# A retention, Mish and squared-ReLU kernel on one core: weights loaded in their own order, odd heads moved by ScalarE, decays broadcast by TensorE, and new constants in the planner

## The chip, the cores and the metric

The kernel runs on one core of one Trainium2 chip. The metric is the device time of one launch in microseconds (us). The kernel before took 871.28 us (median of 3 runs, 869.62 to 871.64). Engines are named as in the profile: PE is TensorE (PEld its weight loads), DVE is VectorE, ACT is ScalarE, POOL is GpSimd, and SP (SyncE) issues every DMA.

## The reference, cut to what matters

```python
# 1. retention: q, k, v of shape (4, 8, 576, 64), float32
scores = (1 / np.sqrt(64)) * np.matmul(q, k.transpose(0, 1, 3, 2))
gamma = 1.0 - 2.0 ** (-5.0 - np.arange(8))
rel = pos[:, None] - pos[None, :]
Dmat = np.where(rel >= 0, gamma[:, None, None] ** rel[None], 0.0)
x = np.matmul(scores * Dmat[None], v)                 # heads side by side: (2304, 512)
# 2. first feed-forward layer: w_in (512, 2048), w_out (2048, 512)
h = x @ w_in
x = (h * np.tanh(softplus(h))) @ w_out                # Mish
# 3. second feed-forward layer, with weights of its own
h = np.maximum(x @ w_in2, 0.0)
out = (h * h) @ w_out2
```

The input weights reach the kernel as the 64-bit words of the host's arrays, and the kernel turns them into float32 itself.

## The kernel before, in words

**Retention.** It goes through 20 steps, five for each batch: four chunks of 128 tokens and a tail of 64. For a step TensorE makes the scores of eight heads (`scores`, L449), VectorE multiplies them with a table of decays (`a`, L458), TensorE makes the outputs from the running state and from the chunk itself (`apply`, L501 and L510) and updates the state (`update`, L471). The keys are scaled with `vdec_sb` (`scale_k`) and the queries with `qdec_sb` (`scale_q`), on VectorE or GpSimd. The table `decay` is made once at the start (`make_decay`): two DMAs repeat a row of `qdec` on all 128 partitions, and eight VectorE instructions (L418) multiply it with a column of `vdec_sb` and the causal mask.

Heads lie in pairs: an even pair has its two heads in partitions 0 to 63 and 64 to 127; for an odd pair `out` gives the upper half of PSUM to the first head and the lower half to the second. ScalarE copies both banks as they are into `part` (two copies a chunk of tokens), so that in `part` the odd pairs have their halves exchanged. To match, the rows of the first layer's `w_in` are loaded with the same exchange by `swapped`: three DMAs, one of 256 KB over all partitions, and two of 128 KB that bring 64 partitions each from the other half. All other weights come as one DMA of 512 KB.

**Weights.** `convert` turns one block of 64-bit words into a float32 tile: a ScalarE copy of the low words (`y`), three VectorE instructions on the high words (`z`, L293 to L295), a VectorE instruction that joins them (`y`, L296), and an addition on VectorE or GpSimd (L297). There are two `raw` buffers, so block i waits until block i-2 has been read. `split_in` and `split_out` cut the tiles into high and low parts for float32r matmuls. Sixteen of the 64 blocks are `w_in` of the first layer.

**Feed-forward layers.** The tokens go in three visits of 768 through four passes over the hidden width, for each of the two layers: 24 visits. `chain` makes seven products for each pair of hidden blocks (L652) in place of eight, with sums of inputs and weights made beforehand; `y_group` makes the second matmul (L702). The split inputs of a visit (`ring`) are kept in DRAM (`keep`) and come back in later passes (`fetch`, 768 KB each).

**The planner.** The order on every engine is made before launch by `Plan`. Each operation has an assumed cost; `due` counts back from when TensorE would need it; `order` simulates the five queues and picks, for each engine, the ready operation that is due first (TensorE only the first ready of the next 14). A DMA costs SP 0.45 us, moves its bytes at an assumed 0.39 MB/us through one queue, and is taken as landed 2.0 us after that. DMAs are issued at most 4 us of queue ahead (`BACKLOG`). Weight DMAs are due 20 us before they are needed (`EARLY`). The engines then run their instructions in the planned order, each with the semaphore waits that its data asks for, so an instruction that waits holds all that stand behind it on its engine.

At the start eleven matmuls on a zero tile (`WARM`) run before the first scores. The launch order asked for there is: step 0, mask, vdec, the decays, step 1, the first 256 columns of `qdec`, steps 2 and 3, the rest of `qdec`; the planner is free to issue them by due time.

Of the kernel before, what the change touches and what calls it, by code (L numbers as in the profile page):

```python
# [54 lines left out]
NEAR = 0.5  # L55
SHARE = 0.8
GATE = 6
EARLY = 20.0
LAST = 14


class Plan:
# [6 lines left out]
    def __init__(self):  # L69
        self.ops, self.wrote, self.read, self.early = [], {}, {}, []  # L70

    def add(self, eng, cost, fn, reads=(), writes=(), moved=0.0, port=False, early=0.0):
# [15 lines left out]
        self.early.append(early)  # L88
        return i

    def due(self):
        due = [1e9] * len(self.ops)
        t = 0.0
        for i, (costs, *_) in enumerate(self.ops):
            if "PE" in costs:
                due[i] = t
                t += costs["PE"]
        for i in range(len(self.ops) - 1, -1, -1):
            for d in self.ops[i][2]:
                costs, _, _, moved, _ = self.ops[d]  # L100
                e = min(costs, key=costs.get)
                c = costs[e] + SEEN[e] + (moved + 2.0 if e == "SP" else 0.0)
                due[d] = min(due[d], due[i] - c)
        return [d - e for d, e in zip(due, self.early)]

    def order(self):
# [6 lines left out]
        free = dict.fromkeys(self.ENGINES, 0.0)  # L113
        ready, start, on = [0.0] * n, [0.0] * n, [None] * n
        waiting = {e: [] for e in self.ENGINES}
# [10 lines left out]
        for i in range(n):  # L126
            if not left[i]:
                release(i)
        queue = 0.0
        for _ in range(n):  # L130
# [3 lines left out]
            for e in self.ENGINES:  # L134
# [3 lines left out]
                if not c:  # L138
                    continue
                now = max(free[e], min(ready[i] for i in c))  # L140
                if e == "SP":
                    now = max(now, queue - BACKLOG)
                can = [i for i in c if ready[i] <= now + 1e-9]
                if e == "POOL":
# [32 lines left out]
            if eng == "SP":  # L177
                queue = max(queue, end) + moved
                end = queue + 2.0
            for u in users[i]:  # L180
                ready[u] = max(ready[u], end + (0.0 if eng == "PE" and "PE" in ops[u][0] else seen))
                left[u] -= 1
                if not left[u]:
                    release(u)
        self.end = max(free.values())
# [10 lines left out]
def kernel(  # L196
# [55 lines left out]

    def dma(out, in_, reads, writes, size, early=0.0):
        fn = lambda: nc.sync.dma_start(out=out, in_=in_)
        plan.add("SP", 0.45, fn, reads, writes, size / 0.39e6, early=early)

    def swapped(out, in_, reads, writes, size, early=0.0):

        a, b = slice(0, D), slice(D, P)
        dma(out[:, 0::2], in_[:, 0::2], reads, writes[:1], size / 2, early)  # L260
        dma(out[a, 1::2], in_[b, 1::2], reads, writes[1:2], size / 4, early)
        dma(out[b, 1::2], in_[a, 1::2], reads, writes[2:], size / 4, early)

# [13 lines left out]
    def convert(i, after=()):  # L277
        g, a = halves[i]
        r, z, y = raw[i % RAWS], zs[i % 2], ys[i % YS]
        kr, kz, ky = [("raw", i % RAWS, j) for j in range(3)], ("z", i % 2), ("y", i % YS)  # L280
        made[g, a] = y, ky
        src = (wp1, wp2)[g // NF].bitcast(U32)[g % NF, a]
        if g < NF and a == 0:
            to, of = (t.rearrange("p (k n) -> p k n", k=KD) for t in (r.rearrange("p n w -> p (n w)"), src))
            swapped(to, of, after, kr, P * DM * 8, EARLY)
        else:
            dma(r.rearrange("p n w -> p (n w)"), src, after, kr, P * DM * 8, EARLY)
        low, hi = r[:, :, 0], r[:, :, 1]
# [140 lines left out]
    def scale_q(s):  # L429
        b, c = steps[s]  # L430
        if not c:
            return
        q, t = heads(s)[:, 0], slice(c * CH, c * CH + size(c))
        either(ALU.mult, q, q, qdec_sb[:, :, t], NP * size(c), [("qdec", int(c > 1)), ("q", s % LD)], [("q", s % LD)])

# [4 lines left out]
    def scores(s):  # L440
# [13 lines left out]
        for e in range(2):  # L454
# [3 lines left out]
                lambda e=e, r=r, d=d: nc.vector.tensor_tensor(a[r, e, :, :n], ps[r, e, :, :n], d, op=ALU.mult),  # L458
                NP * n, [("decay", e), ("sc", s % 2, e)], [("a", s % 2, e)],
            )  # L460
# [22 lines left out]
    def apply(s):  # L483
# [46 lines left out]
    zero = cst.tile([P, 512], F32R, tag="zero", name="zero")  # L530
    warm = pso[2].rearrange("p h t -> p (h t)")
# [37 lines left out]
    def open_late():  # L569
# [18 lines left out]
             + [("e", j) for j in range(ES)] + ["mask", "vdec", "zero"]  # L588
             + [("qdec", i) for i in range(2)] + [("decay", e) for e in range(2)])

# [92 lines left out]
    def y_group(u, th, f):  # L683
# [7 lines left out]
        for i in range(na):  # L691
# [15 lines left out]

            plan.add("PE", 0.52 if m == 0 else 0.69, mm, [kw + (0,), kw + (1,), ("g", j, 0), ("g", j, 1), ky], [ky])
        if f < FPP - 1:
# [138 lines left out]
```

## Time and profile before

| | before |
|---|---|
| median of 3 runs | 871.28 us |
| the profiled execution's own time | 870.46 us |
| its span, first to last instruction | 868.7 us |
| PE busy | 830.3 us (96%) |
| DVE busy | 612.1 us (70%) |
| ACT busy | 404.0 us (47%) |
| POOL busy | 130.1 us (15%) |
| mean granted TensorE clock | 0.986 |
| moved by DMA | 191.94 MB, 221 GB/s |

Busy time is what an engine's instructions cover; DMA-issuing instructions are not in it. Matmuls are pipelined and their ends are modelled, so a busy PE is not a PE at its peak. The span is 1.76 us shorter than the execution's time. Retention takes the first 92 us of the span, the feed-forward layers the rest.

### The profile page before, as it was taken

The numbers are of one execution on the slowest core, as the hardware profiler recorded it, in microseconds if no ns is written. First come the engines' busy times: TensorE is split into PE (matmuls) and PEld (weight loads), VectorE is DVE, ScalarE is ACT, GpSimd is POOL, SyncE is SP. The second block draws the span as 40 slices with busy tenths as digits, with TensorE's granted clock in tenths as the row PEclk, the third lists the DMA queues.
The fourth block names the chain that finished last, engine by engine and source line by source line (L and its number), as shares of the span: only waits on it lengthen the run. The fifth ranks groups of instructions, "written<-read, shape, count | busy, mean of one in ns | idle before, by whom it ended". The sixth has DMA issues, their size and how long they took to land.

```text
span 868.7 us, 13459 instructions
## 1 busy us (share of the span) xinstructions
PE 830.3 (96%) x5195; PEld 774.3 (89%) x5195; DVE 612.1 (70%) x1082; ACT 404.0 (47%) x817; POOL 130.1 (15%) x91
## 2 busy tenths in 40 slices
PE   7877889998999999999999999999999999999998
PEld 6766779998999999999999989888889889889986
DVE  4799999748437673677549998779468964664453
ACT  1423665655335433554347557564344533543331
POOL 1544360011001100112000321110011201000000
PEclk7989999999999999999999999999999999999999
DMA  9988565686375574477357376468348536426621
GB/s 326 325 287 320 204 262 194 243 299 232 120 278 189 186 303 172 156 278 295 125 211 278 107 293 252 151 233 323 122 172 312 195 157 255 177 99 270 263 101 73
DMA packets 50944, 191.94 MB, mean 221 GB/s; under 512 B 5440, under 2 KB 15808, under 8 KB 50880
## 3 DMA queue, kind: packets, MB, share of 16 engines
q1 hardware_dynamic: 50880, 191.08, 60.5%
q8 instruction: 41, 0.67, 0.3%
q14 instruction: 23, 0.19, 0.1%
HBM read 153.31 MB, written 37.75 MB: 220 GB/s over the span
## 4 chain that ended last, share of the span: by engine, by line
PE 68%; DVE 17%; DMA 7%; ACT 3%; issue 3%; POOL 1%; SPq 0%; DVEq 0%; POOLq 0%; ACTq 0%
PE py L702 35%; PE h L652 30%; DMA raw<-in_wp_dram 5%; DVE y L296 2%; DVE g L265 1%; DVE z L293 1%; DVE z L294 1%; DVE a L458 1%; PE o L510 1%; DVE part L725 1%; DVE z L295 1%; DVE y L297 1%; DVE win L250 1%; PE sc L449 1%; DMA kv<-in_kv_dram 1%
## 5 line engine op out<-in xcount | busy, mean ns | idle before, releaser
L652 PE MATMUL h<-ring,win 128*128 128x384 f32 x2016 | 386.4, 337 | 12.8 <-ACT cp L242 9.4
L652 PEld LDWEIGHTS h<-ring,win 128*128 128x128 f32 x2016 | 356.1, 188 | 25.0 <-ACT cp L242 13.1
L702 PE MATMUL py<-g,wout 128*128 128x384 f32 x1152 | 216.6, 335 | 1.6 <-DVE part L725 0.9
L702 PE MATMUL py<-wout,g 128*128 128x512 f32 x864 | 214.8, 393 | 0.0
L702 PEld LDWEIGHTS py<-g,wout 128*128 128x128 f32 x1152 | 200.6, 188 | 3.8 <-DVE part L725 2.1
L702 PEld LDWEIGHTS py<-wout,g 128*128 128x128 f32 x864 | 161.0, 188 | 29.8 <-DVE g L265 0.4
L242 ACT ACTIVATE cp<-h 128x384 f32<-128x384 f32 x144 | 70.8, 492 | 120.4 <-PE h L652 117.5
L265 DVE TENSOR_TENSOR g<-h,g 128x384 fp32r<-128x384 f32 x144 | 79.4, 551 | 31.5 <-ACT g L242 31.2
L297 POOL TENSOR_TENSOR y<-z,y 128x512 uint32<-128x512 uint32 x35 | 51.4, 1469 | 281.8 <-DVE y L296 237.6
L242 ACT ACTIVATE g<-h 128x384 fp32r<-128x384 f32 x144 | 70.6, 491 | 41.0 <-DVE h L611 39.1
L635 DVE TENSOR_TENSOR e<-h,cp 128x384 f32<-128x384 f32 x48 | 26.6, 554 | 76.6 <-ACT cp L242 76.6
L725 DVE TENSOR_TENSOR part<-py,part 128x384 f32<-128x384 f32 (+1 forms) x126 | 73.3, 606 | 6.5 <-PE py L702 5.4
L635 DVE TENSOR_TENSOR h<-h,cp 128x384 f32<-128x384 f32 x96 | 53.9, 562 | 31.5 <-PE h L652 30.6
L242 ACT ACTIVATE h<-h 128x384 f32<-128x384 f32 x72 | 34.2, 476 | 67.2 <-DVE h L635 54.6
L242 ACT ACTIVATE e<-h 128x384 f32<-128x384 f32 x72 | 35.2, 489 | 52.6 <-DVE h L635 45.9
L242 ACT ACTIVATE y<-raw 128x512 f32<-128x512 uint32 x64 | 43.0, 671 | 28.8 <-DVE wout L250 8.8
L296 DVE SCALAR_TENSOR_TENSOR y<-raw,y 128x512 uint32<-128x512 uint32 x64 | 45.9, 721 | 7.5 <-ACT y L242 7.5
L293 DVE TENSOR_SCALAR z<-raw 128x512 uint32<-128x512 uint32 x64 | 31.3, 489 | 26.7 <-DMA raw<-in_wp_dram 26.5
L611 DVE SCALAR_TENSOR_TENSOR h<-h,e 128x384 f32<-128x384 f32 x72 | 40.3, 560 | 11.4 <-ACT e L242 11.3
L250 POOL TENSOR_TENSOR win<-y,win 128x512 fp32r<-128x512 f32 x9 | 12.1, 1349 | 223.8 <-ACT win L242 220.0
L265 DVE TENSOR_TENSOR g<-e,g 128x384 fp32r<-128x384 f32 x48 | 29.4, 612 | 19.6 <-ACT g L242 19.6
L242 ACT ACTIVATE e<-e 128x384 f32<-128x384 f32 x48 | 25.2, 524 | 31.8 <-DVE e L635 31.8
(51 smaller groups left out, 649.7 us busy)
## 6 DMA issues: line engine op xcount, KB each, us to landing
ring<-d SPq DMA_DIRECT2D x126, 768.0 KB, 6.7
d<-ring SPq DMA_DIRECT2D x42, 768.0 KB, 5.2
raw<-in_wp_dram SPq DMA_DIRECT2D x48, 512.0 KB, 3.6
qk<-in_qk_dram SPq DMA_DIRECT2D x16, 512.0 KB, 7.4
kv<-in_kv_dram SPq DMA_DIRECT2D x16, 512.0 KB, 7.7
out_dram<-part SPq DMA_DIRECT2D x18, 256.0 KB, 2.1
raw<-in_wp_dram SPq DMA_DIRECT2D x16, 256.0 KB, 3.7
raw<-in_wp_dram SPq DMA_DIRECT2D x32, 128.0 KB, 4.7
```

The costliest lines, as they stand in the source:

```text
L242: fn = lambda: nc.scalar.activation(out() if callable(out) else out, in_() if callable(in_) else in_, func, **kw)
L250: fn = lambda eng: eng.tensor_tensor(get(out), a, get(b).bitcast(F32), op=op)
L265: return lambda: eng.tensor_tensor(out, a, b.bitcast(F32), op=ALU.subtract)
L293: dve(lambda: ts(z, hi, 0x7FFFFFFF, None, op0=band), 256, kr, [kz], True)
L294: dve(lambda: ts(zf, zf, HI_MIN, HI_MAX, op0=ALU.max, op1=ALU.min), 256, [kz], [kz], True)
L296: dve(lambda: stt(yu, hi, 0x80000000, yu, op0=band, op1=bor), 512, kr + [ky], [ky], True)
L297: add = lambda eng: eng.tensor_tensor(yu, z, yu, op=ALU.add)
L611: lambda: nc.vector.scalar_tensor_tensor(ph(), ph(), 0.0, e(), op0=ALU.max, op1=ALU.mult),
L635: lambda: nc.vector.tensor_tensor(dst(), bank(b)(), late["cp"][j], op=ALU.add),
L652: nc.tensor.matmul(dst(), w[:, hw, wi, s], ring[i][:, hx, k], start=(new and k == 0 and n == 0), stop=(k == 1 and n == 2), skip_group_chec ...
L702: nc.tensor.matmul(y, st[:, a], mv[:, b], start=(f == 0 and k == 0), stop=(f == FPP - 1 and k == 2), skip_group_check=True,)
L725: lambda dst=dst, y=y: nc.vector.tensor_tensor(dst, y(), dst, op=ALU.add),
```

## The change: what it does

The outputs of odd pairs still lie exchanged in PSUM, but ScalarE now moves them: the even bank is copied as before, and the odd bank by two copies, low half from high half and the reverse. `part` then has all heads in their own order, `w_in` of the first layer comes by one DMA like the other weights, and `swapped` is gone. The decays' rows come from `qdec_sb`, whose first part is now the first chunk alone; TensorE repeats a row over 128 partitions with a column of ones, into the second scores bank, and VectorE reads it there. In the planner: DMA at 0.36 MB/us, landing 2.4 us later, at most 8 DMAs not landed, weight blocks taken as ready 3 us after landing (`SLACK`), and any operation of ACT, DVE or POOL with over 8 us to spare starts at the earliest 1.5 us after its inputs (`CALM`, `AMPLE`). Two assumed TensorE costs are new.

```diff
+CALM = 1.5
+AMPLE = 8.0
+SLACK = 3.0
+LAND = 2.4
+OPEN = 8
...
-                c = costs[e] + SEEN[e] + (moved + 2.0 if e == "SP" else 0.0)
+                c = costs[e] + SEEN[e] + (moved + LAND if e == "SP" else 0.0)
...
-        queue = 0.0
+        queue, landed = 0.0, [0.0] * OPEN
...
-                now = max(free[e], min(ready[i] for i in c))
+                now = max(free[e], min(calm[i] for i in c))
                 if e == "SP":
-                    now = max(now, queue - BACKLOG)
-                can = [i for i in c if ready[i] <= now + 1e-9]
+                    now = max(now, queue - BACKLOG, landed[-OPEN])
+                can = [i for i in c if calm[i] <= now + 1e-9]
...
                 queue = max(queue, end) + moved
-                end = queue + 2.0
+                landed.append(queue + LAND)
+                end = queue + LAND + self.slack[i]
...
+                    spare = due[u] + late - ready[u]
+                    rest = spare > AMPLE and "PE" not in ops[u][0] and "SP" not in ops[u][0]
+                    calm[u] = ready[u] + CALM * rest
...
-        plan.add("SP", 0.45, fn, reads, writes, size / 0.39e6, early=early)
-
-    def swapped(out, in_, reads, writes, size, early=0.0):
-
-        a, b = slice(0, D), slice(D, P)
-        dma(out[:, 0::2], in_[:, 0::2], reads, writes[:1], size / 2, early)
-        dma(out[a, 1::2], in_[b, 1::2], reads, writes[1:2], size / 4, early)
-        dma(out[b, 1::2], in_[a, 1::2], reads, writes[2:], size / 4, early)
+        plan.add("SP", 0.45, fn, reads, writes, size / 0.36e6, early=early, slack=slack)
...
-        if g < NF and a == 0:
-            to, of = (t.rearrange("p (k n) -> p k n", k=KD) for t in (r.rearrange("p n w -> p (n w)"), src))
-            swapped(to, of, after, kr, P * DM * 8, EARLY)
-        else:
-            dma(r.rearrange("p n w -> p (n w)"), src, after, kr, P * DM * 8, EARLY)
+        dma(r.rearrange("p n w -> p (n w)"), src, after, kr, P * DM * 8, EARLY, SLACK)
...
     def load_qdec(i):
-        t = slice(0, 2 * CH) if i == 0 else slice(2 * CH, S)
+        t = slice(0, CH) if i == 0 else slice(CH, S)
...
     def make_decay():
         for e in range(2):
-            row = qdec[D * e : D * e + 1, :, :CH].to_broadcast([P, NP, CH])
-            dma(decay[:, e], row, (), [("decay", e)], P * 2048)
-        for e in range(2):
+            at, r = psc[1][:, e], slice(D * e, D * e + 1)
+            def mm(at=at, r=r):
+                for hp in range(NP):
+                    nc.tensor.matmul(at[:, hp], ones[r], qdec_sb[r, hp, :CH], start=(hp == 0), stop=True, skip_group_check=True)
+            plan.add("PE", 0.9, mm, ["ones", ("qdec", 0)], [("sc", 1, e)])
             for hp in range(NP):
                 t, w = decay[:, e, hp], vdec_sb[:, 0, 2 * hp + e : 2 * hp + e + 1]
                 dve(
-                    lambda t=t, w=w: nc.vector.scalar_tensor_tensor(t, t, w, mask_sb, op0=ALU.mult, op1=ALU.mult),
-                    CH, ["mask", "vdec", ("decay", e)], [("decay", e)], True,
+                    lambda t=t, w=w, b=at[:, hp]: nc.vector.scalar_tensor_tensor(
+                        t, b, w, mask_sb, op0=ALU.mult, op1=ALU.mult
+                    ),
+                    CH, ["mask", "vdec", ("sc", 1, e)], [("decay", e, hp)],
                 )
...
-            for j in range(2):
-                dst, src = part[v][:, j::2, w : w + m], po[j][:, : NP // 2, c0 : c0 + m]
+            low, high = slice(0, D), slice(D, P)
+            for j, r, t in ((0, slice(0, P), slice(0, P)), (1, low, high), (1, high, low)):
+                dst, src = part[v][r, j::2, w : w + m], po[j][t, : NP // 2, c0 : c0 + m]
...
+    plan.add("DVE", 0.2, lambda: nc.vector.memset(ones, 1.0), (), ["ones"])
     for _ in range(WARM):
-        plan.add("PE", 0.36, mm, ["zero"], [("o", 2)])
+        plan.add("PE", 0.42, mm, ["zero"], [("o", 2)])
...
+    load_qdec(0)
     make_decay()
     load_step(1)
-    load_qdec(0)
...
-            plan.add("PE", 0.52 if m == 0 else 0.69, mm, ...)
+            plan.add("PE", 0.52 if m == 0 else 0.694, mm, ...)
```

## Rows read from the trace of the kernel before

**Rows 1.** Busy us by stretch (start:end, length, PE, PEld, DVE, ACT, POOL, PEclk, DMA share, GB/s):
```profile
0.00:10.00 10.00, 5.83 (x27) 4.41 (x27) 1.18 (x2) 1.28 (x1) 0.20 (x4) 0.95 0.80 244
10.00:20.00 10.00, 9.79 (x102) 8.16 (x104) 7.51 (x16) 1.53 (x4) 1.91 (x2) 0.53 1.05 393
20.00:39.00 19.00, 18.80 (x404) 16.64 (x400) 14.76 (x19) 8.73 (x23) 10.44 (x9) 1.00 1.05 342
39.00:92.40 53.40, 37.50 (x641) 31.17 (x637) 50.51 (x71) 20.17 (x52) 25.25 (x16) 0.90 0.90 310
92.40:130.00 37.60, 31.95 (x167) 30.35 (x168) 35.92 (x50) 24.52 (x49) 19.88 (x11) 0.95 0.58 212
...
200.00:220.00 20.00, 16.96 (x94) 15.84 (x93) 15.84 (x31) 9.66 (x21) 3.34 (x3) 1.00 0.86 304
...
270.00:310.00 40.00, 38.32 (x216) 36.84 (x215) 29.33 (x59) 19.57 (x39) 6.75 (x5) 1.00 0.70 233
...
490.00:510.00 20.00, 18.84 (x92) 15.83 (x91) 20.00 (x33) 13.12 (x25) 5.56 (x4) 1.00 0.70 281
510.00:690.00 180.00, 177.54 (x881) 159.20 (x880) 141.09 (x260) 93.86 (x186) 25.53 (x18) 1.00 0.58 214
```

**Rows 2.** Waits of the whole span (engine, line, releaser: us in total, times, longest):
```profile
DVE z L293 <- DMA raw<-in_wp_dram: 26.5, 18, 4.2
...
PE h L652 <- ACT cp L242: 9.4, 9, 2.4
...
PE o L501 <- ACT part L242: 7.5, 4, 3.5
```

**Rows 3.** Chain that ended last, pieces in order (start us, us, what):
```profile
3.85 6.84 DMA mask_sb<-in_mask_dram
...
10.81 2.79 DVE decay L418 x8
...
34.89 7.91 DMA kv<-in_kv_dram
```

**Rows 4.** The same chain from 178 to 312 us, its longest pieces:
```profile
186.34 8.59 DMA raw<-in_wp_dram
...
284.19 8.81 DMA raw<-in_wp_dram
```

**Rows 5.** PE from 0 to 45 us, in order (start, us, idle before):
```profile
6.12 1.16 PE L449 MATMUL sc<-qk 64*128 64x128 f32 x16
10.01 1.12 PE L471 MATMUL st<-kv 128*64 128x64 f32 x16 [2.73 <-DVE kv L250]
...
42.70 0.66 PE L501 MATMUL o<-qk,sbd 64*64 64x128 f32 x12 [3.51 <-ACT part L242]
```

**Rows 6.** Busy us by stretch, as in Rows 1:
```profile
46.00:48.00 2.00, 1.02 (x12) 0.83 (x10) 1.95 (x5) 0.00 (x0) 0.47 (x1) 0.84 1.03 408
55.00:60.00 5.00, 3.17 (x32) 2.60 (x34) 5.00 (x6) 1.66 (x4) 2.05 (x2) 0.69 1.06 257
```

**Rows 7.** Instructions by line and form, 0 to 92.4 us:
```profile
L242 ACT ACTIVATE part<-o 128x256 f32<-128x256 f32 x28 | 9.8, 379 | 12.1 <-PE o L510 11.9
...
L242 ACT ACTIVATE part<-o 128x128 f32<-128x128 f32 x16 | 3.3, 277 | 10.6 <-PE o L510 10.6
```

**Rows 8.** DMA issues, 0 to 120 us (xcount, KB each, median us to landing):
```profile
raw<-in_wp_dram SPq DMA_DIRECT2D x5, 256.0 KB, 5.5
raw<-in_wp_dram SPq DMA_DIRECT2D x10, 128.0 KB, 5.3
...
decay<-in_qdec_dram SPq DMA_DIRECT2D x2, 256.0 KB, 6.0
```

**Rows 9.** SP's queue, 24 to 55 us (start, us):
```profile
24.41 0.58 SPq L254 DMA_DIRECT2D raw<-in_wp_dram  x1
...
36.19 2.14 SPq L254 DMA_DIRECT2D raw<-in_wp_dram  x2
...
51.25 3.15 SPq L254 DMA_DIRECT2D raw<-in_wp_dram  x5
```

More of the change, by code (lines that the diff above doesn't have):

```diff
@@ L69, in __init__, with add @@
     def __init__(self):
-        self.ops, self.wrote, self.read, self.early = [], {}, {}, []
-    def add(self, eng, cost, fn, reads=(), writes=(), moved=0.0, port=False, early=0.0):
+        self.ops, self.wrote, self.read, self.early, self.slack = [], {}, {}, [], []
+    def add(self, eng, cost, fn, reads=(), writes=(), moved=0.0, port=False, early=0.0, slack=0.0):
         i = len(self.ops)
@@ L88, in add @@
         self.early.append(early)
+        self.slack.append(slack)
         return i
@@ L113, in order @@
         free = dict.fromkeys(self.ENGINES, 0.0)
-        ready, start, on = [0.0] * n, [0.0] * n, [None] * n
+        ready, start, on, calm = [0.0] * n, [0.0] * n, [None] * n, [0.0] * n
         waiting = {e: [] for e in self.ENGINES}
@@ L251, in either, with dma @@
         plan.add("ANY", dict(DVE=0.07 + n * 0.00104, POOL=0.15 + n * 0.0024), fn, reads, writes, port=True)
-    def dma(out, in_, reads, writes, size, early=0.0):
+    def dma(out, in_, reads, writes, size, early=0.0, slack=0.0):
         fn = lambda: nc.sync.dma_start(out=out, in_=in_)
-        plan.add("SP", 0.45, fn, reads, writes, size / 0.39e6, early=early)
-    def swapped(out, in_, reads, writes, size, early=0.0):
-        a, b = slice(0, D), slice(D, P)
-        dma(out[:, 0::2], in_[:, 0::2], reads, writes[:1], size / 2, early)
-        dma(out[a, 1::2], in_[b, 1::2], reads, writes[1:2], size / 4, early)
-        dma(out[b, 1::2], in_[a, 1::2], reads, writes[2:], size / 4, early)
+        plan.add("SP", 0.45, fn, reads, writes, size / 0.36e6, early=early, slack=slack)
     def minus(eng, out, a, b):
@@ L279, in convert @@
         r, z, y = raw[i % RAWS], zs[i % 2], ys[i % YS]
-        kr, kz, ky = [("raw", i % RAWS, j) for j in range(3)], ("z", i % 2), ("y", i % YS)
+        kr, kz, ky = [("raw", i % RAWS)], ("z", i % 2), ("y", i % YS)
         made[g, a] = y, ky
         src = (wp1, wp2)[g // NF].bitcast(U32)[g % NF, a]
-        if g < NF and a == 0:
-            to, of = (t.rearrange("p (k n) -> p k n", k=KD) for t in (r.rearrange("p n w -> p (n w)"), src))
-            swapped(to, of, after, kr, P * DM * 8, EARLY)
-        else:
-            dma(r.rearrange("p n w -> p (n w)"), src, after, kr, P * DM * 8, EARLY)
+        dma(r.rearrange("p n w -> p (n w)"), src, after, kr, P * DM * 8, EARLY, SLACK)
         low, hi = r[:, :, 0], r[:, :, 1]
@@ L433, in scale_q @@
         q, t = heads(s)[:, 0], slice(c * CH, c * CH + size(c))
-        either(ALU.mult, q, q, qdec_sb[:, :, t], NP * size(c), [("qdec", int(c > 1)), ("q", s % LD)], [("q", s % LD)])
+        either(ALU.mult, q, q, qdec_sb[:, :, t], NP * size(c), [("qdec", 1), ("q", s % LD)], [("q", s % LD)])
     def keys(s, e):
@@ L458, in scores @@
                 lambda e=e, r=r, d=d: nc.vector.tensor_tensor(a[r, e, :, :n], ps[r, e, :, :n], d, op=ALU.mult),
-                NP * n, [("decay", e), ("sc", s % 2, e)], [("a", s % 2, e)],
+                NP * n, [("decay", e, hp) for hp in range(NP)] + [("sc", s % 2, e)], [("a", s % 2, e)],
             )
@@ L530 @@
     zero = cst.tile([P, 512], F32R, tag="zero", name="zero")
+    ones = cst.tile([P, P], F32, tag="ones", name="ones")
     warm = pso[2].rearrange("p h t -> p (h t)")
     plan.add("DVE", 0.5, lambda: nc.vector.memset(zero.bitcast(F32), 0.0), (), ["zero"])
+    plan.add("DVE", 0.2, lambda: nc.vector.memset(ones, 1.0), (), ["ones"])
     for _ in range(WARM):
         mm = lambda: nc.tensor.matmul(warm, zero[:, :P], zero, start=True, stop=True)
-        plan.add("PE", 0.36, mm, ["zero"], [("o", 2)])
+        plan.add("PE", 0.42, mm, ["zero"], [("o", 2)])
     load_step(0)
@@ L588 @@
              + [("e", j) for j in range(ES)] + ["mask", "vdec", "zero"]
-             + [("qdec", i) for i in range(2)] + [("decay", e) for e in range(2)])
+             + [("qdec", i) for i in range(2)] + [("decay", e, hp) for e in range(2) for hp in range(NP)] + ["ones"])
     visits = [(m, p, v) for m in range(2) for p in range(NPASS) for v in range(NSB)]
@@ L706, in mm @@
                     )
-            plan.add("PE", 0.52 if m == 0 else 0.69, mm, [kw + (0,), kw + (1,), ("g", j, 0), ("g", j, 1), ky], [ky])
+            plan.add("PE", 0.52 if m == 0 else 0.694, mm, [kw + (0,), kw + (1,), ("g", j, 0), ("g", j, 1), ky], [ky])
         if f < FPP - 1:
```

## The prediction

> **What bounds the kernel now.** I read the table of busy time by stretch first. PE is busy 830.3 of 868.7 us, so 38.4 us of idle is all there is to save, beside stretches at a low clock. The rows of the table say where that idle lies [rows 1]: 4.2 us before 10 us, 15.9 us from 39 to 92.4, 5.7 us from 92.4 to 130, and then in lumps, 3.0 us (200 to 220), 1.7 (270 to 310), 1.2 (490 to 510), 2.5 (510 to 690), with none to speak of between. The last 4 us of idle stand behind the last matmul and the change does not touch them. So retention holds half of the idle, and the rest comes at the starts of passes.
>
> The limit is not one engine. From 10 to 39 us the DMA engines are full (share 1.05) and PE hardly waits. From 39 to 92.4 us VectorE is busy 50.5 of 53.4 us, while ScalarE has 20.2 and DMA a share of 0.90: there VectorE sets the pace [rows 1].
>
> The chain of waits, read next, gives the joints. In the first 43 us it goes through the mask's DMA (landed 6.84 us after it could start), the eight decay instructions, then PE, and then a `kv` DMA issued at 34.89 that takes 7.91 us to land [rows 3]. In the last of these PE sits idle 3.51 us; the row names ScalarE's copy of outputs [rows 5], which was queued behind a conversion of weights whose data were late. In the feed-forward layers the chain leaves PE only through weight DMAs of 8.59 and 8.81 us [rows 4], after which VectorE works off a queue for some ten microseconds until PE waits on a ScalarE copy. The table of waits has the same in sum: VectorE stood 26.5 us in 18 waits, 4.2 at most, in front of a weight block that had not landed, and PE's largest wait is 9.4 us on `cp` [rows 2]. An order fixed in advance that believed the data would be there sooner is what these rows have in common.
>
> **The change, part by part.** *The decays.* Two DMAs of 256 KB go [rows 8]. The parts of `qdec` have the same bytes as before in sum. That is 0.524 MB less in the stretch where the engines are full: at the 408 GB/s of a clean stretch [rows 6], 1.3 us. PE gets eight matmuls (16 records, as the scores have): 1.16 us at the full clock by the row of the first scores, double that at half. They need the smaller `qdec` DMA, which can go out first. Cover is there: PE idles 2.73 us after the first scores [rows 5]. Without that cover the cost is 1.2 to 2.3 us. VectorE has the same eight instructions, 2.79 us [rows 3], now from PSUM; I take no difference, bounds -0.4 and +0.8. The mask is on the chain and its DMA stands behind some 2 MB; with 0.25 to 0.8 MB less ahead of it, it lands 0.6 to 2 us earlier. Between 10 and 20 us PE's granted clock is 0.53, half of its 2.4 GHz level, after the 2.73 us gap [rows 1, 5]. If the decay matmuls fill that gap, the 9.8 us of PE work there could shrink by up to 4.9 us. I price this at nothing, because the DMA engines are full from 10 us on and set what comes after; the 4.9 us is a bound.
>
> *The weights.* Each `w_in` block of the first layer was three DMAs, 256 KB and twice 128 KB [rows 8]. SP issues 32 DMAs fewer, about 0.6 us each [rows 9]; the chain goes through transfers and not through their issue, so that is nothing. What the pieces cost the DMA engines shows where they are dense. Just after five pieces were issued [rows 9], the engines were full (1.06) at 257 GB/s; another full stretch, without them, ran at 408 [rows 6]. In 5 us, 1.29 MB that needed 3.15 us: 1.85 us lost, for two blocks (these five pieces and the one before), 0.9 us a block. Two blocks, six pieces in all, were issued before the late `kv` DMA and beside it [rows 3, 9]: 1.85 us. With the decays, 3.1 us less is in front of that DMA, and the stall behind it is 3.5 us, so this fits into it. I take 3.1; the bounds are 0 and 4. The later blocks give 0.9 us each where VectorE sets the pace, and I count them at nothing.
>
> Here the Trainium skill speaks against the change. "DMA: Bandwidth & Descriptors", section Specifications, gives 512 B as the smallest transfer at line rate. A swapped block moves runs of 1 KB by the kernel's layout, so by that rule its removal gives nothing and the retention term would be the 1.3 us of the decays alone. The same skill's "SBUF — State Buffer", section on the DMA port swizzle, says that 64 partitions reach half of the ports, which fits the low rate in the trace. The rows at 257 against 408 GB/s decide for me; the first rule is a rival below.
>
> *ScalarE's copies.* There were 28 copies of 256 columns and 16 of 128, two for a chunk [rows 7], so 22 chunks and 22 copies more: 14 by 0.379 and 8 by 0.277 us, 7.5 us. No row shows a copy between halves; I take the price of the straight one, since a copy's time follows its columns in the two rows; bounds 0 (if they ran wholly beside others) and 7.5 us, all of it on the path. ScalarE is busy 20.2 of 53.4 us, so most is hidden by idle time. What is queued behind the third copy is the state's copy and the weights' first step, and PE waits for the former. PE did wait 7.5 us on such copies, in four waits [rows 2]. I put 0.4 us there and 0.3 us where the last copy of retention stands before the first product: +0.7.
>
> *The planner.* Slack of 3 us, a later landing, a lower rate and at most 8 open DMAs move the conversion of weights behind other work. VectorE's mean wait for a block was 1.5 us (26.5/18) and the longest 4.2 [rows 2]: 3.4 us more cover all but the longest. The limit of 8 open DMAs can hold SP, and behind it stand the loads of later steps and the `ring` tiles; in the dense stretch the engines have work enough meanwhile, so I take nothing. What stalls PE after 130 us is 8.3 us (3.0 + 1.7 + 1.2 + 2.5) [rows 1]. The chain says that late blocks start these lumps, but VectorE's queue, 15.8 of 20 us from 200 to 220 and 20.0 of 20 from 490 to 510, carries them on, and no work is taken from it. I take 3.5 of the 8.3; bounds -8.3 and +5, the latter the worst case of a reshuffled order (one more lump as in 200 to 220 and 270 to 310). In the first visit (92.4 to 130), 5.7 us of idle, I expect no gain: the calm time holds back the very conversions it waits for, unless they have under 8 us to spare.
>
> The sum: -3.1 + 0.7 - 3.5 = -5.9 us on the profiled execution's 870.46 us, which is 0.8 below the median. 864.6 us.
>
> **The rivals.** *The slack costs more than it saves.* There are two raw buffers; each block now holds one for 3 us more by plan, and with calm on the copy and the `z` steps 3 to 6 us more. Eight blocks have to be through before the first visit can end, four rounds over two buffers: 4 x 3 = 12 us later in the plan. Once that passes the idle that is there anyway (5.7 us), 6 us is new stall, and with the +0.7 of the copies and -3.1 of the DMAs, +3.6 to +6: 874 to 876. For: VectorE is busy 35.9 of 37.6 us in that stretch [rows 1], with no room to catch up. Against: blocks with less than 8 us to spare get no calm, and the DMA is due 20 us early. It decides from the point where the second half of `win` or the first `wout` is ready after the first visit's products ask for it.
>
> *VectorE takes the gain back.* From 39 us it is full; if its work, not the late `kv`, sets 92.4, retention ends where it did, and if the lumps only move, the time is 870 to 871. For: 95% busy. Against: the chain enters VectorE's run through that DMA.
>
> *More falls.* The clock holds and PE starts 2 us sooner, and 7 of the 8.3 us go: -3.1 - 2 + 0.7 - 7 + 2 of the first visit's idle = -13.4, 857. For: every lump has the same trigger. Against: VectorE's queue.
>
> *Runs of 1 KB cost nothing.* Then retention gives 1.3 in place of 3.1: 866.4. The two rates in the trace speak against it. "DMA: Bandwidth & Descriptors" of the Trainium skill speaks for it.
>
> **How the numbers follow.** The forecast has 0.38 (861 to 866), the case of 1 KB runs 0.10, more falls 0.22, VectorE 0.13, the slack 0.17. About 0.3% (2.6 us) is what a measurement of this kernel can tell from no change, so 868.7 to 873.9 is "the same". Faster: 0.38 + 0.10 + 0.22 = 0.70; same: 0.13, less the half that could end either way, 0.12; slower: 0.18. The range of 8 in 10 runs from 855, a little under the case where more falls, to 874, where the slack begins to cost; for the likeliest case alone it is 861 to 866.
>
> **What would show it.** Right: the weight DMAs of the first layer show 512 KB only and full stretches from 20 to 60 us stay over 330 GB/s; the first product starts near 90 us; VectorE's waits for weight blocks fall under 10 us; the lumps after 130 us sum to about 5. Wrong: retention ends at 92 or later (VectorE or the copies), or idle from 92 to 130 us grows over 8 us (the slack), or PE's waits on copies of outputs pass 10 us.

## The result, and the profile after

Measured beside each other, the kernel before took 871.46 us and the changed kernel 859.8 us (medians; 858.3 to 862.08 in four runs): a ratio of 0.9871, 95% interval 0.9844 to 0.9898, so 11.7 us faster. The profiled execution took 858.3 us, with a span of 856.5.

The page's line of busy times, of the changed kernel:

```profile
PE 827.6 (97%) x5211; PEld 775.9 (91%) x5211; DVE 599.3 (70%) x1100; ACT 403.5 (47%) x839; POOL 109.0 (13%) x74
```

The stretches of [rows 1], now of the changed kernel (length, then busy us and count of PE, PEld, DVE, ACT, POOL, then PE's granted clock, DMA share, GB/s):

```profile
0.00:10.00 10.00, 7.80 (x45) 6.09 (x47) 1.50 (x5) 1.28 (x1) 0.20 (x4) 0.98 0.78 268
10.00:20.00 10.00, 9.05 (x124) 7.98 (x126) 6.59 (x15) 2.69 (x8) 3.60 (x3) 0.68 1.04 406
20.00:39.00 19.00, 17.95 (x399) 15.76 (x398) 15.56 (x25) 12.54 (x33) 9.24 (x8) 1.00 1.04 350
39.00:92.40 53.40, 41.23 (x656) 35.26 (x652) 50.09 (x74) 27.60 (x67) 22.90 (x15) 0.90 0.86 301
92.40:130.00 37.60, 31.20 (x151) 29.15 (x150) 35.05 (x52) 24.28 (x50) 16.72 (x8) 0.82 0.60 217
200.00:220.00 20.00, 20.00 (x117) 20.00 (x116) 14.53 (x31) 9.92 (x22) 1.29 (x1) 1.00 0.84 328
270.00:310.00 40.00, 40.00 (x233) 40.00 (x232) 27.82 (x56) 19.71 (x40) 5.67 (x4) 1.00 0.69 271
490.00:510.00 20.00, 20.00 (x100) 17.87 (x100) 19.85 (x35) 12.71 (x25) 2.01 (x1) 1.00 0.87 334
510.00:690.00 180.00, 179.97 (x895) 161.75 (x894) 131.45 (x257) 90.30 (x182) 17.68 (x12) 1.00 0.60 225
```

Between 39 and 92.4 us PE works 3.7 us more than before; in the four late stretches it has no idle time to speak of, where it had 8.3 us (after 130 us as a whole it has 2.3 us, nearly all at 489.06). From 92.4 to 130 it has 6.4 us of idle in place of 5.7. VectorE is as full as before in both early stretches.

Waits of the changed kernel, which answer to [rows 2]; no wait of VectorE for a weight block is listed any more:

```profile
PE h L660 <- ACT cp L252: 5.4, 3, 2.5
PE o L506 <- DVE qk L260: 5.1, 2, 4.5
PE py L710 <- DVE wout L260: 3.0, 1, 3.0
```

PE of the changed kernel in order (start, us; in brackets the idle time before and its releaser), to be read beside [rows 5]:

```profile
6.33 1.71 PE L415 MATMUL sc<-qdec_sb,ones 1*128 1x128 f32 x16
...
38.14 0.61 PE L506 MATMUL o<-qk,sbd 64*64 64x128 f32 x14
...
42.32 0.69 PE L476 MATMUL st<-kv 128*64 128x64 f32 x16
...
86.64 13.82 PE L660 MATMUL h<-ring,win 128*128 128x384 f32 x78 [1.00 <-ACT part L252]
112.94 2.66 PE L660 MATMUL h<-ring,win 128*128 128x384 f32 x6 [2.49 <-ACT cp L252]
...
121.45 12.57 PE L710 MATMUL py<-g,wout 128*128 128x384 f32 x60 [2.99 <-DVE wout L260]
...
489.06 1.28 PE L660 MATMUL h<-ring,win 128*128 128x384 f32 x6 [2.31 <-ACT cp L252]
```

The stall of 3.51 us at 42.70 is gone: the same product runs at 38.14 with no idle time in front of it. The first product of the feed-forward starts at 86.64 in place of 92.4, and of the late lumps one is left, at the change of layers.

To compare kernels I split PE's time at four points of its own order, the same in all: the start of the ninth state product (48.76 us before, 42.32 after), the first product, the end of the first visit (taken as 40 us of products), and the end of the products. What is lost after the first product is the start of a product less the work ahead of it at the undisturbed pace: 2.08 us for 12 products of 384 columns, 2.08 for 9 of 512. All in us, each from one trace (those of the experiments are told below):

```
kernel                     ninth state   from there to    lost in       lost   sum of
                           product at    first product    first visit   later  the four
before                        48.8           43.6            8.9        14.3    115.6
after                         42.3           44.3           11.9         5.0    103.6
e1_old_plan                   46.8           39.2            8.7        11.3    106.1
e10_old_land                  45.7           40.1            9.6         9.4    104.8
e2_new_plan                   44.0           43.1           21.1         5.0    113.3
e3_no_calm                    44.2           44.4           12.3         4.5    105.4
e4_no_slack                   41.7           40.4           12.7         3.6     98.3
e5_decay_only                 47.4           39.8            9.4        15.7    112.3
e6_unswap_only                49.7           40.3            9.1        10.8    109.9
e7_no_copies                  47.5           44.6            5.5        14.1    111.7
e8_no_slack_no_pool           42.2           33.2           11.0         2.1     88.5
e11_before_no_pool            46.4           34.9           12.0         5.1     98.4
e12_old_no_pool               43.7           35.9            7.6         2.1     89.3
```

Of the 12.0 us between the first two rows, 6.5 come before the ninth state product, 9.3 from the late lumps, and 3.0 are paid in the first visit; 0.7 more is lost between the ninth state product and the first one of the feed-forward. By this measure 14.3 us were lost later in the kernel before, of which 8.3 stand as idle time in [rows 1]. Each trace is one run: that of e1 took 860.84 us, 2.9 above the median told below, and that of e11 853.47, 4.0 under it, so their sums differ from the medians by as much.

### The profile page after: what moved, and what is told of

Read it like the earlier page. It is cut to its first block, busy times and chain, and to the rows that moved or that the text cites. A ratio compares the mean times of both kernels' runs of the same rounds, so it can differ in the third digit from the quotient of the medians.

```text
span 856.5 us, 13403 instructions
## 1 busy us (share of the span) xinstructions
PE 827.6 (97%) x5211; PEld 775.9 (91%) x5211; DVE 599.3 (70%) x1100; ACT 403.5 (47%) x839; POOL 109.0 (13%) x74
## 4 chain that ended last, share of the span: by engine, by line
PE 82%; DVE 3%; ACT 1%; issue 0%
PE py L710 45%; PE h L660 37%; DVE part L733 1%; DVE g L268 0%; DVE ring L260 0%; DVE wout L260 0%; DVE h L643 0%; DVE e L619 0%; DVE z L293 0%; ACT g L252 0%; DVE h L619 0%; ACT e L252 0%; DVE part L350 0%; DVE t L351 0%; DVE win L260 0%
## 5 line engine op out<-in xcount | busy, mean ns | idle before, releaser
L710 PEld LDWEIGHTS py<-g,wout 128*128 128x128 f32 x1152 | 202.8, 189 | 3.7 <-DVE wout L260 3.5
L733 DVE TENSOR_TENSOR part<-py,part 128x384 f32<-128x384 f32 (+1 forms) x126 | 75.2, 609 | 81.6 <-PE py L710 81.4
L295 DVE SCALAR_TENSOR_TENSOR y<-raw,y 128x512 uint32<-128x512 uint32 x64 | 49.8, 779 | 0.4 <-ACT y L252 0.4
L296 POOL TENSOR_TENSOR y<-z,y 128x512 uint32<-128x512 uint32 x19 | 29.6, 1560 | 154.3 <-DVE y L295 87.5
L260 POOL TENSOR_TENSOR win<-y,win 128x512 fp32r<-128x512 f32 x9 | 12.3, 1371 | 273.9 <-ACT win L252 219.5
L268 DVE TENSOR_TENSOR g<-e,g 128x384 fp32r<-128x384 f32 x48 | 33.0, 688 | 2.2 <-ACT g L252 2.2
L252 ACT ACTIVATE part<-py 128x384 f32<-128x384 f32 (+1 forms) x42 | 22.4, 539 | 21.3 <-PE py L710 20.7
```

Of the source, the lines that this page charges most:

```text
L252: fn = lambda: nc.scalar.activation(out() if callable(out) else out, in_() if callable(in_) else in_, func, **kw)
L260: fn = lambda eng: eng.tensor_tensor(get(out), a, get(b).bitcast(F32), op=op)
L268: return lambda: eng.tensor_tensor(out, a, b.bitcast(F32), op=ALU.subtract)
L295: dve(lambda: stt(yu, hi, 0x80000000, yu, op0=band, op1=bor), 512, kr + [ky], [ky], True)
L296: add = lambda eng: eng.tensor_tensor(yu, z, yu, op=ALU.add)
L710: nc.tensor.matmul(y, st[:, a], mv[:, b], start=(f == 0 and k == 0), stop=(f == FPP - 1 and k == 2), skip_group_check=True,)
```

## Experiments

Theory A: the planner's numbers brought the gain. Theory B: the structure did (weights in one piece, the third copy, the decays on TensorE). Each ratio is against the kernel before on the same chip. The edits are shown condensed.

**Structure alone and planner alone.** e1 is the changed kernel with the planner's old numbers; e2 is the kernel before with the new ones and the code that uses them.

```diff
 # e1_old_plan: after, and PE's assumed costs 0.36 and 0.69 as before
-CALM, SLACK, LAND, OPEN = 1.5, 3.0, 2.4, 8 ;  size / 0.36e6
+CALM, SLACK, LAND, OPEN = 0.0, 0.0, 2.0, 4000 ;  size / 0.39e6
 # e2_new_plan: before
-end = queue + 2.0 ;  size / 0.39e6
+end = queue + LAND + self.slack[i] ;  size / 0.36e6 ;  CALM, SLACK, LAND, OPEN as after
```

> The changed kernel with the planner's old numbers (0.39 MB/us, landing 2.0 us, no limit on open DMAs, no slack, no calm, the old two TensorE costs): the weights, ScalarE's copies and the decays are as changed. Theory A (the new numbers of the planner removed the lumps after 130 us): the first product starts near 88 us, but PE loses 10 us or more again between 130 us and the end, and the time is 866 to 870 us. Theory B (fewer and fuller DMAs did it, the numbers little): the lumps stay away, 858 to 862 us.

> The kernel before with all new numbers of the planner alone; weights still come exchanged in three pieces, decays by DMA, two copies a chunk. Theory A: after 130 us PE loses under 6 us, as in the changed kernel, and retention ends near 92 us as before: 862 to 866 us. Theory B: the lumps of the kernel before stay, 868 to 873 us.

The structure alone took 857.93 us (0.9839, 0.9811 to 0.9866), the planner's numbers alone 867.53 (0.9944, 0.9927 to 0.9961). So by the time B holds: the structure brings 14.3 us, and the new numbers on top of it nothing that can be told from zero (0.9871 against 0.9839, with intervals that overlap). But what was expected of A's late lumps came true as well: e1 loses 11.3 us after the first visit, e2 only 5.0, as the changed kernel does. The new numbers do remove most of the late lumps, and what they gain there they lose elsewhere. e2's trace shows why its gain is small, first as a stretch, then as PE's row:

```profile
92.40:130.00 37.60, 22.96 (x125) 21.03 (x123) 37.08 (x57) 24.33 (x49) 13.49 (x8) 0.89 0.65 229
```

```profile
131.36 8.93 PE L712 MATMUL py<-g,wout 128*128 128x384 f32 x40 [10.43 <-DVE wout L260]
```

VectorE waits for a weight block once in the whole span (0.5 us, against 26.5 before), the stall at 42 us and the late lumps are gone, 4.8 and 9.3 us by the table; and PE then stands in the first visit for 12.2 us more, 10.43 of them in front of one converted `wout`.

**The planner's terms one by one**, from the changed kernel:

```diff
 # e3_no_calm
-CALM = 1.5
+CALM = 0.0
 # e4_no_slack
-SLACK = 3.0
+SLACK = 0.0
```

> The changed kernel without the calm time (0 in place of 1.5 us). If calm is what keeps VectorE's queue free for urgent work, the losses after 130 us come back in part (+3 us or more: 863 us and up). If slack does it, no change there; and if calm delayed the weights of the first visit, that visit loses 3 us less than the changed kernel's 11.9, which makes 856 to 858 us.

> The changed kernel without the slack (weight blocks taken as ready when they should have landed, not 3 us later). If VectorE standing before late weight blocks made the lumps, that wait rises from almost nothing to 15 us or more in sum and the time to 863 to 867 us. If slack is only what delayed the first visit, the first visit loses 3 to 6 us less and the time is 854 to 857 us.

Without calm: 859.91 us (0.9847, 0.9817 to 0.9876), no difference that can be measured. Without slack: 853.23 (0.9776, 0.9753 to 0.9799), 6.6 us less than with it. The first visit stays as it was (12.7 us lost, 11.9 with slack); the gain is 3.9 us between the ninth state product and the first product, and 1.4 later. The late lumps do not come back, so slack is not needed to remove them, and by e3 (4.5 us lost later) neither is calm. The other numbers (rate, landing, at most 8 open DMAs) were not taken apart.

To see how far the order by itself moves the time, e1 again with a landing 0.1 us later:

```diff
 # e10_old_land, from e1_old_plan
-LAND = 2.0
+LAND = 2.1
```

> The changed kernel with the planner's old numbers, as in the first run, but DMAs are taken as landed after 2.1 us in place of 2.0: a number so little changed that no mechanism of this study is in it. What it moves is what a reshuffled order moves by itself. If that is small, the time is within 1.5 us of that run's 857.9 us; if the parts of this change do not add up because each one reshuffles the order, it is off by 2 to 5 us, to either side.

It took 859.62 us (0.9845, 0.9798 to 0.9893), 1.7 us above e1, and its columns moved by -1.1, +0.9, +0.9 and -1.9. Runs of e1 itself lie between 857.15 and 860.84 us, so these differences need not all be the order's; but 2 us in a column, or in the time, cannot be put down to a part of the change.

**The structure's parts**, each from the kernel before with the old planner numbers. e5 has the decays on TensorE and the new parts of `qdec`; e6 the one-piece weights with the three copies; e7 is e6 with the old two straight copies; it leaves out the exchange of the odd heads' halves.

```diff
 # e5_decay_only: before
-dma(decay[:, e], row, (), [("decay", e)], P * 2048)
+nc.tensor.matmul(at[:, hp], ones[r], qdec_sb[r, hp, :CH], ...)
 # e6_unswap_only: before
-swapped(to, of, after, kr, P * DM * 8, EARLY)
+dma(to, of, after, kr, P * DM * 8, EARLY)      # and the copies of after
 # e7_no_copies: e6_unswap_only
-for j, r, t in ((0, slice(0, P), slice(0, P)), (1, low, high), (1, high, low)):
+for j in range(2):                             # all 128 partitions, straight
```

> The kernel before with the decays broadcast by TensorE (and the qdec parts cut as in the change) and nothing else new: old planner numbers, exchanged weights, two copies a chunk. Theory C (the start decides: the decay matmuls keep TensorE's clock up and the mask lands sooner): the half-clock stretch between 10 and 20 us is gone or shorter, the first product starts 2 to 5 us before 92.4, and the time is 866 to 869 us. Theory D (the weights' pieces were what filled the DMA engines): retention ends within 1.5 us of 92.4, 870 to 872 us.

> The kernel before with weights loaded in one piece and three copies a chunk, and nothing else new. Theory D: retention ends 3 us sooner or more and lumps after 130 us shrink, since nine of sixteen exchanged blocks come after retention: 861 to 867 us. Theory C: 869 to 872 us.

> As the run with the weights in one piece alone, but with the two straight copies a chunk of the kernel before: odd heads are not moved (left out), so that only the price of the third copy differs. If the 22 copies cost what the prediction took (0.7 us), this is 0.5 to 1 us faster than that run; if they lie on the path, 3 to 7 us faster; if they are wholly hidden, the same within 0.5 us, apart from what a new order does.

e5 took 868.45 us (0.9954, 0.9932 to 0.9976), 3.9 less than before; e6 864.22 (0.9904, 0.9874 to 0.9934), 8.1 less; e7 865.05 (0.9916, 0.9886 to 0.9947). The third copies cost nothing that can be measured. e6 and e7 also show how losses wander: their sums differ by 1.8 us, three of their columns by 3 to 4, with the same weights in both. The parts make 12.0 us, together they make 14.3; the difference is of the size that e10 shows for an order.

Both parts gain at a place that I had not named, and not at the one that I had. First the stall of [rows 5] itself: its product on PE in e5, e6, e1 and e2, one after the other.

```profile
41.03 1.12 PE L517 MATMUL o<-qk,sbd 64*64 64x128 f32 x12 [3.74 <-ACT part L252]
```

```profile
44.00 1.12 PE L500 MATMUL o<-qk,sbd 64*64 64x128 f32 x12 [4.47 <-ACT part L252]
```

```profile
41.95 0.65 PE L506 MATMUL o<-qk,sbd 64*64 64x128 f32 x12 [2.41 <-ACT part L252]
```

```profile
39.53 0.61 PE L511 MATMUL o<-qk,sbd 64*64 64x128 f32 x14
```

With fewer bytes (e5) or no exchanged pieces (e6) in front of the late `kv` DMA the stall is as long as before or longer; with both (e1) 2.41 us of it are left; with the old structure and the new planner numbers (e2) it is gone. ScalarE's rows show why, two of the kernel before, then one of e6 and one of e2:

```profile
40.97 0.67 ACT L242 ACTIVATE y<-raw 128x512 f32<-128x512 uint32 x1 [3.69 <-DMA raw<-in_wp_dram]
...
42.27 0.37 ACT L242 ACTIVATE part<-o 128x256 f32<-128x256 f32 x1
```

```profile
42.27 0.84 ACT L252 ACTIVATE ring<-t 128x768 fp32r<-128x768 f32 x1 [4.55 <-DVE t L349]
```

```profile
38.45 0.66 ACT L252 ACTIVATE part<-o 128x256 f32<-128x256 f32 x2 [1.31 <-PE o L520]
```

In the kernel before, the copy of outputs that PE needs stands in ScalarE's order behind the first step on a weight block, which waits 3.69 us for its data. In e6 it stands behind a `ring` copy that waits 4.55 us for VectorE. In e2 neither stands there: the copies of outputs wait for PE alone.

The gain that I had not named comes later. The parts gain 3.8 and 3.3 us, from the ninth state product to the first product: e1, e4, e5, e6 and e10 have 39 to 40 us there, the kernels with slack and the one before 43 to 44. But e7, with e6's weights, has 44.6, so that this gain belongs to the parts, and not to the order that each brings, is not shown.

**What an exchanged block costs.** e9 leaves all the computation out, writes zeros, and moves 24 weight blocks of 0.524 MB in each of four ways: one DMA; the three pieces of `swapped`; two pieces over 128 partitions in runs of 1 KB; two pieces of 64 partitions with whole rows.

```diff
+if kind == 0: dma(out=flat, in_=src)
+elif kind == 1: ...                              # even, and two exchanged halves, as in swapped
+elif kind == 2: dma(out=to[:, 0::2], in_=of[:, 0::2]); dma(out=to[:, 1::2], in_=of[:, 1::2])
+else: dma(out=flat[lo], in_=src[lo]); dma(out=flat[up], in_=src[up])
```

> Transfers alone, nothing else is computed (zeros are written as the output): four stages of 24 weight blocks of 512 KB each, with a pause between. Stage 1 one DMA a block, stage 2 the three exchanged pieces, stage 3 two pieces with runs of 1 KB on all 128 partitions, stage 4 two pieces of 64 partitions with whole 4 KB rows. If the prediction's 0.9 us a block holds, stage 2 takes about 22 us more than stage 1 (some 31 us). If it is the half of the partitions, stage 4 is slow and stage 3 is not; if it is the runs of 1 KB, the reverse. If pieces cost nothing, all four are alike.

Windows of e9, one inside each way (length, busy us of DVE, which only clears the tiles, and of POOL, PE's clock, DMA share, GB/s):

```profile
5.00:24.00 19.00, 13.53 (x16) 0.00 (x0) 1.00 1.02 411
36.00:70.00 34.00, 15.50 (x17) 0.00 (x0) 1.00 1.05 263
84.00:118.00 34.00, 20.65 (x23) 0.00 (x0) 1.00 1.10 348
126.00:172.00 46.00, 19.02 (x22) 0.00 (x0) 1.00 1.04 239
```

At a full share of the DMA engines, the rates are 411, 263, 348 and 239 GB/s: 1.28, 1.99, 1.51 and 2.19 us a block. In this window an exchanged block costs 0.72 us more than a straight one. Its rate was not steady, as two parts of the second way show:

```profile
40.00:60.00 20.00, 10.03 (x11) 0.00 (x0) 1.00 1.09 274
60.00:80.00 20.00, 7.35 (x9) 0.00 (x0) 1.00 1.04 228
```

By these it costs 0.64 to 1.02 us more. Two pieces in runs of 1 KB cost 0.23; two pieces of 64 partitions cost 0.91. Both ways also make two DMAs of a block; what that alone costs no run shows.

**GpSimd beside VectorE.** e4 to e6 pointed to VectorE's stretch, where its instructions are not all of one length. VectorE and POOL of the changed kernel, 100 to 106 us:

```profile
100.97 2.16 POOL L260 TENSOR_TENSOR ring<-t,ring 128x768 fp32r<-128x768 f32 x1 [4.41 <-ACT ring L252]
101.00 0.42 DVE L292 TENSOR_SCALAR z<-raw 128x512 uint32<-128x512 uint32 x1
101.34 2.07 DVE L294 TENSOR_SCALAR z<-z 128x512 uint32<-128x512 uint32 x1
103.09 2.03 POOL L260 TENSOR_TENSOR ring<-part,ring 128x768 fp32r<-128x768 f32 x1
103.33 2.34 DVE L295 SCALAR_TENSOR_TENSOR y<-raw,y 128x512 uint32<-128x512 uint32 x1
105.30 2.08 POOL L260 TENSOR_TENSOR ring<-part,ring 128x768 fp32r<-128x768 f32 x1 [0.18 <-ACT ring L252]
105.60 2.07 DVE L293 TENSOR_SCALAR z<-z 128x512 f32<-128x512 f32 x1
```

The steps on `z` at 101.34 and 105.60 take 2.07 us, and each ends 0.3 us after a GpSimd instruction. That they need 0.42 us by themselves is the row of the first of them in e8, the kernel without GpSimd's work that is told next (busy us, then mean ns of one):

```profile
L294 DVE TENSOR_SCALAR z<-z 128x512 uint32<-128x512 uint32 x64 | 26.5, 418 | 0.0
```

Not every instruction beside GpSimd is lengthened: the step at 101.00 took 0.42 us, though GpSimd's row starts at 100.97 (times on POOL are rough). Before the first product the instructions that are 0.25 us or more above short ones of their kind hold 17.9 us in excess in the kernel before (16 of them), 12.9 in the changed one, 11.3 in e5. So I took all element-wise work that may go to either engine off GpSimd, in the kernel before (e11), in e1 (e12) and in e4 (e8).

```diff
 # e8_no_slack_no_pool, e11_before_no_pool, e12_old_no_pool
-plan.add("ANY", dict(DVE=0.07 + n * 0.00104, POOL=0.15 + n * 0.0024), fn, reads, writes, port=True)
+plan.add("DVE", 0.07 + n * 0.00104, fn, reads, writes, port=True)
-plan.add("ANY", dict(DVE=0.6, POOL=1.4), add, [kz, ky], [ky], port=True)
+plan.add("DVE", 0.6, add, [kz, ky], [ky], port=True)
```

> The changed kernel without slack and with every operation that VectorE or GpSimd may take given to VectorE. If VectorE's 2 us instructions in the first visit (0.4 to 1 us elsewhere) come from GpSimd running beside them, they vanish, the first visit loses 4 us or more less than the 12.7 of the run without slack, and the time is 847 to 851 us. If GpSimd carries work that VectorE has no time for, retention ends later by 3 us or more and the time is 854 to 860 us.

> The kernel before with every operation that VectorE or GpSimd may take given to VectorE, and nothing else. If GpSimd beside VectorE was what made retention and the lumps slow in both kernels, this gains about what it gave the changed kernel without slack (10 us): 860 to 864 us, VectorE's 2 us instructions are gone, and the lumps after 130 us shrink. If that gain needs the change, it is 867 to 873 us.

> The changed kernel with the planner's old numbers and nothing on GpSimd. If the planner's slack-free new numbers matter once VectorE's durations are as the planner takes them, this is 4 us or more slower than the run with them (842.8 us), with waits for weight blocks of 15 us in sum; if they matter no longer, it is within 2 us of it.

e8 took 842.78 us (0.9659, 0.9626 to 0.9693), e11 857.48 (0.9806, 0.9754 to 0.9857), e12 844.12 (0.9664, 0.9608 to 0.9719). e8 and e11 gained more than was expected. The page's busy times, of the kernel before and of e11:

```profile
PE 830.3 (96%) x5195; PEld 774.3 (89%) x5195; DVE 612.1 (70%) x1082; ACT 404.0 (47%) x817; POOL 130.1 (15%) x91
```

```profile
PE 822.7 (97%) x5195; PEld 770.6 (90%) x5195; DVE 613.6 (72%) x1169; ACT 405.7 (48%) x817; POOL 0.2 (0%) x4
```

VectorE does 87 instructions more, those of GpSimd, in the same busy time: the 130 us of POOL cost it as much as the work itself. One group shows it, `kv` scaled in SBUF, 0 to 92.4 us, in the kernel before and in e11:

```profile
L250 DVE TENSOR_TENSOR kv<-kv,vdec_sb 128x512 f32<-128x512 f32 x14 | 15.0, 1070 | 11.3 <-DMA vdec_sb<-in_vdec_dram 7.9 <-DMA kv<-in_kv_dram 3.4
```

```profile
L250 DVE TENSOR_TENSOR kv<-kv,vdec_sb 128x512 f32<-128x512 f32 x16 | 11.0, 689 | 15.3 <-DMA vdec_sb<-in_vdec_dram 7.8 <-DMA kv<-in_kv_dram 7.4
```

The mean falls from 1070 to 689 ns, in no one of the three kernels without GpSimd is there a lengthened instruction before the first product, and the stretch from the ninth state product shrinks to 33 to 36 us.

The late lumps shrink too, and not because the weight blocks come sooner. VectorE's waits for weight blocks in e1, e12 and e11:

```profile
DVE z L292 <- DMA raw<-in_wp_dram: 19.6, 13, 3.4
```

```profile
DVE z L292 <- DMA raw<-in_wp_dram: 21.9, 21, 2.5
```

```profile
DVE z L293 <- DMA raw<-in_wp_dram: 26.6, 19, 3.8
```

With the waits as they were, the loss after the first visit falls from 11.3 us (e1) to 2.1 (e12), and from 14.3 (before, with 26.5 us of waits) to 5.1 (e11). So late weight blocks alone do not make the lumps; here they did it only with GpSimd's work beside VectorE. Taking that work off also brings a new order, and these runs do not separate the two.

The gain adds to that of the structure: 14.2 us by itself (e11), and from e11 to e12 the structure brings 13.4 more, as it brought 14.3 with GpSimd at work. From e4 to e8 it is 10.4. e8 beats both kernels; e8 and e12 cannot be told apart, so the planner's other new numbers are worth nothing measurable there.

## Why the prediction came out as it did

The direction was right and the time lies in the range (855 to 874), but the forecast's size was half: -5.9 us forecast, -11.7 measured, nearer to the case in which more falls (857). That case was summed with a wrong sign: with +2 for the first visit its terms make -9.4, and -13.4 and 857 follow only with -2. Of its terms the lumps came true (7 of 8.3 us of idle forecast, 6.0 measured after 130 us), the clock held only in part (0.68 from 10 to 20 us), and the first visit lost 3.0 us in place of gaining 2.

*The DMA term (-3.1) failed as a mechanism.* The prediction put the saved bytes and pieces in front of the late `kv` DMA and subtracted them from the stall of 3.5 us. e5 and e6 save them and keep the stall (3.74 and 4.47 us). The `kv` transfer landed at 42.80 (34.89 + 7.91, [rows 3]), when the stall had just ended; what stood in front of PE was a weight block's first step in ScalarE's order. What removes it is the order: the planner's new numbers alone bring the ninth state product from 48.8 to 44.0 us. The price of a block, 0.9 us worked out from two stretches [rows 6, 9], was right, 0.64 to 1.02 measured; where it is worth something was wrong. The later blocks, which I counted at nothing, fall in the stretch in which VectorE sets the pace, and there e6 gained 3.3 us, though e7 with the same weights gained nothing there.

On the rule that spoke against the change: by the Trainium skill, "DMA: Bandwidth & Descriptors", section Specifications, runs of 1 KB would be at line rate. e9 disagrees in part, with 348 against 411 GB/s, though as two DMAs a block in place of one. The skill's "SBUF — State Buffer", section on the DMA port swizzle, has 64 partitions reach half of the ports; the 239 GB/s of the fourth way, 0.58 of the first, agree with it in kind. An estimate from e9: half of an exchanged block moves in pieces of 64 partitions, and half of 0.91 us is the larger part of the 0.72.

*The decays (-1.3) were worth 3.9 us alone.* The clock, which I priced at nothing with a bound of 4.9, belongs here: in e5 the granted clock stayed at 1.00 from 10 to 20 us, 2.4 GHz, where it was 0.53 [rows 1]. The two rows, of e5:

```profile
10.00:20.00 10.00, 8.18 (x153) 6.86 (x152) 8.41 (x16) 2.47 (x7) 4.40 (x4) 1.00 1.04 404
```

```profile
36.90 0.39 PE L517 MATMUL o<-qk,sbd 64*64 64x128 f32 x4
```

PE reaches this product 1.9 us sooner than before (38.80). Most of the part's gain is again in VectorE's stretch (39.8 in place of 43.6 us). That the clock caused the 1.9 us is not shown: in e6 it was 0.85 in that stretch and PE was no sooner. Nor does the filled gap alone hold it: the changed kernel has decay products there too, and 0.68.

*The copies (+0.7)* cost nothing that e6 against e7 can show. The price of one was right: between halves it is 379 ns in e6, as for a straight copy [rows 7].

```profile
L252 ACT ACTIVATE part<-o 64x256 f32<-64x256 f32 x28 | 10.6, 379 | 0.6
```

*The planner (-3.5 of the late lumps, no gain in the first visit).* This term was too small: the idle time after 130 us fell from 8.3 to 2.3 us, and by the table the lumps lost 9.3 us of 14.3, as VectorE's waits for weight blocks went from 26.5 us to none listed. That the late blocks start the lumps was only half of it: e11 and e12 keep these waits and lose 5.1 and 2.1 us. The first visit lost 3.0 us more, the side on which the slack rival stood, but not through slack: without it the visit loses 12.7, without calm 12.3, with all old numbers 8.7, so the loss belongs to the other new numbers or to the order that they bring. The slack does cost, 6.6 us in all, and more than half of it in the stretch before the first product, where VectorE is full and the rival did not look.

*The assumption behind all terms* was that VectorE's busy time from 39 us on is work. Part of it was waiting for GpSimd inside the instruction: e11 does all of both engines' work in the same VectorE time. The rival in which VectorE takes the gain back rested on the same reading.

Of the signs named in advance: the weight DMAs are single ones of 512 KB (64 of them), the full stretches from 20 to 50 us ran at 355, 350 and 377 GB/s (from 50 to 60 the engines were no longer full, share 0.78), the first product started sooner than 90 us, the waits for weight blocks fell under 10 us, and the idle after 130 us fell to 2.3, under the 5 named. PE's idle in the visit, 6.4 us, stayed under the 8 that would have spoken for the slack.

Open remains which of the new numbers takes the stall and the lumps away (rate, landing and open limit were not tried alone; e3 and e4 show that calm or slack can be left out), and how much of each part's gain is its own work rather than the order that it brings about.

## What to carry to other kernels

A busy engine is not an engine at work: compare an instruction's duration alone with that beside its neighbour before you call its time given, and try the neighbour's work on it. Before you subtract saved bytes from a stall, read the rows of the engine that ends it: here what PE waited for stood behind something else in ScalarE's order, and the saved bytes did not remove the stall. With an order planned ahead, test each part alone, and count 2 us of the time, and up to 4 us of a single stage, as what the order alone can do (e6 and e7). New numbers in a plan can pay in one stage and be paid for in another: in e2 9.3 us in the late lumps against 12.2 in the first visit. The slack paid nowhere that e4 shows.

## What the runs showed of the hardware that was not expected

- VectorE and GpSimd: instructions of 0.42 us took 2.07 beside a GpSimd `tensor_tensor` of 2.0 to 2.2 us and ended 0.3 us after it. The Trainium skill, "SBUF — State Buffer", section "Who interferes with whom", describes the pair of ports that both share as a lock held for a whole instruction; the pairs of rows that end one just behind the other agree with that.
- DMA: two pieces of 64 partitions, issued one behind the other on one queue, moved 239 GB/s at a share of 1.04; the halves did not add up to the 411 GB/s of one DMA over 128 partitions.
- TensorE: repeating a row over 128 partitions by eight one-row products took 1.71 us (1.91 in e5), where the prediction's row for the first scores had 1.16.
